# Attention and two dense layers on one core: four token blocks of 256 to 512 become three of 512, and the units are gone through to and fro

## The chip, the core and the metric

The kernel runs on one core of one Trainium2 chip. The core has TensorE (PE: matrix products, into PSUM), VectorE (DVE), ScalarE (ACT), GpSimd (POOL) and SyncE (SP, which issues the transfers). The time of a run is device microseconds from the first to the last instruction of the program and what lies around it. Three runs of the kernel before took 701.15 to 702.93 us, median 701.39.

## What is computed

Attention over a sliding window with a few sink tokens, then two dense layers over the same 1536 tokens:

```
q, k, v: (2, 8, 768, 64)            # batch, heads, tokens, head size
scores = q k^T / 8                  # kept: first n_sink = 4 keys, and the last window = 128 keys
x  = softmax(scores) v              # -> 1536 tokens x 512
h  = x @ w_in1                      # 512 x 2048
g  = (a0 + a1 h + a2 h^2 + a3 h^3) / (1 + |b0||h| + |b1|h^2 + 1e-6)
x2 = g @ w_out1                     # 2048 x 512
h  = x2 @ w_in2                     # layer 2, the same sizes
out = (h * sigmoid(1.702 h)) @ w_out2
```

The weights arrive as 64-bit floats.

## The kernel before

**Tiling.** The tokens are cut into blocks T0 to T3 (`TB`, line 31) of 256, 384, 384 and 512 tokens; a block is a list of 128-token query blocks of one or two sequences. The 2048 hidden columns are 16 chunks of 128 in two halves of 8 (`HALVES`). A unit is one layer `m`, one block and one half (`UNITS`, line 35): for each layer, first half with T0 to T3, then second half with T0 to T3, 16 units in all. A step is as many chunks as fill 512 columns of the block: two chunks for T0, one for the others.

**A step.** `g1` (first products) makes `h` = x w_in for the chunk: 12 products per chunk, since operands are split in a high and a low part (`xh`, `xl`; a weight tile `wi` or `wo` holds both parts of one chunk). `el_a` and `el_b` turn `h` into `gh` and `gl` on ScalarE and VectorE: in layer 1 with seven VectorE operations (tiles `s`, `z`, `gh`, `gl`; the one that writes `gl` is the last), in layer 2 with two. `g2` (second products) adds the chunk's share of g w_out to four accumulators `acc`: in layer 1 again 12 products as wide as the block, in layer 2 with tokens as rows and always 512 columns wide. `g2` of a step follows `g1` of the third step after it (`LAG`).

**Partial sums.** A unit sees 8 of 16 chunks. At its end `finish` copies the four accumulators to a tile `xf`; after the second half they are added to `xf` on VectorE, and the sum is split into the next layer's `xh` and `xl` or sent out. If the unit is the block's only one in that layer (`part is None` at the last unit), the accumulators are copied once to a tile of tag `r`, and nothing is added.

**Weights.** 64 weight tiles (16 chunks, `wi` and `wo`, two layers) are transferred into two buffers `wraw` and decoded from 64-bit by `decode`: on VectorE five operations a tile (`dy`, two kinds of `dt`, and the one that writes the low part of `wi` or `wo`), on ScalarE one or two. There are 8 slots each for `wi` and `wo` and one more once attention is over, so a chunk of the next half can be decoded only when the last product with an old chunk frees its slot. I call the block with which that happens the turning block: T3 before, for both turns within a layer and for the turn between layers.

**Attention.** `attention(T, ...)` makes the layer-1 input of block T, head by head: scores on TensorE (`k`,`q`), masks and maxima on VectorE (`m`, `nm`), exponentials on ScalarE, normalisation on GpSimd, transposes (`ident`,`a`) and values (`th`,`vr`) on TensorE. The first product of layer 1 needs all 8 heads of T0. Until then, and while TensorE's list has holes, the planner puts in fillers: products with a tile of zeros (line 844), 110 of them, beside 20 at the start (line 565).

**Order.** All operations go through one planner (`Program.play`), which fixes the order on every engine when the program is built: each operation has a cost, the one with the longest tail goes first, and `BIAS`, `HEAD` and `THETA` (numbers per category of operation) shift that. TensorE, VectorE, ScalarE, GpSimd and SyncE then run their lists strictly in that order.

Of the kernel before, what the change touches and what calls it, by code (L numbers as in the profile page):

```python
# [27 lines left out]
LN2_64 = 64.0 * 0.6931471805599453  # L28


TB = [[(0, [0, 1])], [(0, [2, 3, 4])], [(0, [5]), (1, [0, 1])], [(1, [2, 3, 4, 5])]]
XF_EARLY = (0, 1)

HALVES = [list(range(NF // 2)), list(range(NF // 2, NF))]
UNITS = [(m, T, fs) for m in (0, 1) for fs in HALVES for T in range(len(TB))]
GROUP = 3
LAG = 3

# [7 lines left out]
TH, SN, PE_OUT = "act/dve", "pool/dve", "act/dve"  # L46

BIAS = {
# [3 lines left out]
}  # L52
HEAD = (0.46, 1.43, 4.3, 7.1)
THETA = 1.27

WARM, FILL, FILL_AHEAD = 20, 6000, 0.1

# [4 lines left out]

START, PE_START, TICK, TICK_COLUMNS = 5.75, 6.25, 10.24 / 3, 3060
PE_LAT = 0.2
COL_FIX, COL_EACH = 0.4, 0.0275
TABLE = 1.3
LAT = 0.16
DMA_LAT, DMA_RATE, DMA_MIN = 1.9, 0.36e6, 65536
# [69 lines left out]
class Program:  # L138
# [139 lines left out]
    def play(self):  # L278
# [92 lines left out]
        def spares(o, e):  # L371
# [3 lines left out]
            for t, i in own[p]:  # L375
                if t >= -o.prio:
                    break
                q += ops[i].alts[p][0]
            return max(free[p], now) + q + o.alts[p][0] > now + o.alts[e][0] + THETA

# [112 lines left out]
def emit(tc, qT, kX, vL, w_in, w_out, ca, cb, nw, out):  # L493
    nc = tc.nc
    R = Program(nc, tc)
# [12 lines left out]
    def hi(eng, o, i):  # L508
        l = eng.split("/")
        return one_of([form(e, o, i) for e in l])  # L510
# [28 lines left out]
    pre_w = {("wraw", j): cst.tile([P, 512, 2], I32, name=f"wraw_{j}") for j in range(RAW_BUFS)}  # L539
    (b0, l0), = TB[0]  # L540
    n0 = len(l0)
# [78 lines left out]
    def moe(pools, blocks, units, x1_ready, late_pool):  # L620
# [153 lines left out]
        def finish(u, m, T, c, a, nt):  # L774
            w = nt if m == 0 else 512
            part = xf.get((m, T, c))
            if u != last_unit[m, T]:
                if part is None:
                    if (m, T) not in xf:
                        early = T in XF_EARLY  # L780
                        xf[m, T] = R.tile(xp if early else get_late, [P, KC * nt], F32, tag=f"xf{T}", name="xf", bufs=1, late=not early)
# [46 lines left out]
    def build_banded():  # L828
        with (
# [22 lines left out]
            def attention(T, xs, alone):  # L852

                parts = TB[T]
                qs = [(b, qb) for b, l in parts for qb in l]
# [30 lines left out]
                for k in sorted(kbs, key=lambda k: -len(near[k])) + (["s"] if sq else []):  # L886
                    w = len(near[k]) if k != "s" else 1
# [15 lines left out]
                def pst(kind):  # L903
                    if alone and kind == "s":
                        return R.tile(ps, [P, 512], F32, tag="acc", name="pss", bufs=4)
                    if alone and kind == "v":
                        return R.tile(ps, [P, 512], F32, tag="h", name="psv", bufs=H_BUFS)
                    return R.tile(ps, [P, 512], F32, tag="att", name="psa", bufs=8 - 4 - H_BUFS)
# [18 lines left out]
                def scores(h):  # L927

                    kr, qr = st.pop(("kq", h // 2))
                    t = []  # L930
                    for e in (h, h + 1):
                        a = R.tile(ap, [P, 4, 2 * P + SC], F32, tag="a", name="a", bufs=A_BUFS)
                        nm = R.tile(ap, [P, 4], F32, tag="nm", name="nm", bufs=5)
                        sm = R.tile(ap, [P, 4], F32, tag="sm", name="sm", bufs=5)
                        st["a", e] = a, sm
                        t.append((slice((e % 2) * D, (e % 2 + 1) * D), a, nm, sm))
                    for i, (b, qb) in enumerate(qs):
                        off, w = (P + SC, P) if qb == 0 else (0, 2 * P + SC)
                        k0 = kcol[b, max(0, qb - 1)] * KW
                        ps_ = [pst("s") for _ in t]  # L940
                        R.op("tensor", "matmul", alloc=[x for y in t for x in y[1:]], cost=w / 600 + 2 * COL_EACH, calls=[
                            dict(out=p[:, :w], lhsT=qr[r, i * P:(i + 1) * P], rhs=kr[r, k0:k0 + w], start=True, stop=True)
                            for p, (r, _, _, _) in zip(ps_, t)])
                        for p, (_, a, nm, sm) in zip(ps_, t):
                            mt = R.tile(ap, [P, 2 * P + SC], F32, tag="m", name="mt", bufs=M_BUFS)
                            R.op("vector", "tensor_tensor_reduce",
                                out=mt[:, :w], in0=p[:, :w], in1=mk[min(qb, 2)], scale=-SCALE, scalar=3.0e38,
                                op0=ALU.add, op1=ALU.min, accum_out=nm[:, i:i + 1])
                            R.op("scalar", "activation", out=a[:, i, off:off + w], in_=mt[:, :w], func=AF.Exp, scale=-1.0,
                                 bias=nm[:, i:i + 1], accum_out=sm[:, i:i + 1])  # L950
# [42 lines left out]
                def values(h):  # L993

                    x = pst("v")
                    calls, vrs = [], []
                    for e in (h, h + 1):
                        r0 = (e % 2) * D
                        p, tr, vr = x[r0:r0 + D], st.pop(("T", e)), st.pop(("v", e))
                        vrs.append(vr)  # L1000
                        ops = []
                        for k in first + later:
                            (g, at), n = place[k], len(near[k])
                            q0 = qcol[near[k][0]]
                            ops.append((p[:, q0 * P:(q0 + n) * P], vr[:, vcol[k], :], tr[g][:, at * P:(at + n) * P]))
                        for j, (o, l, r) in enumerate(ops):
                            calls.append(dict(out=o, lhsT=l, rhs=r, start=(j == 0), stop=(not sq and j == len(ops) - 1)))
                    if sq:
                        for e in (h, h + 1):
                            q0, n = qcol[sq[0]] * P, len(sq) * P  # L1010
                            calls.append(dict(out=x[(e % 2) * D:(e % 2 + 1) * D, q0:q0 + n], lhsT=vrs[e % 2][:SC, vcol[sq[0][0], "s"], :], rhs=st.pop(("sT", e))[:, :n], start=False, stop=True))
                    cost = COL_FIX + sum(c["rhs"].n / 1200 + COL_EACH for c in calls)
                    R.op("tensor", "matmul", calls=calls, cost=cost)
                    n, c = nq * P, h // 2
                    hi(XH, xs[0][c][:, :n], x[:, :n])
                    lo("dve", xs[1][c][:, :n], x[:, :n], xs[0][c][:, :n])
# [4 lines left out]
                def first_of(h):  # L1021
# [3 lines left out]
                    if h:  # L1025
                        R.follow(firsts[-2], firsts[-1], 2 * HEAD[T])

# [8 lines left out]

            moe((wp, xp, gp, tp, ps), TB, UNITS, attention, late_pool)
            held.pop().__exit__(None, None, None)

    def build_general():  # L1040
        with tc.tile_pool(name="xd", bufs=1, space=DRAM) as dp:
# [66 lines left out]
            with (  # L1108
# [8 lines left out]
                def x1_ready(T, xs, alone):  # L1117
                    n = sum(len(l) for _, l in TB[T]) * P
                    t0 = TB[T][0][0] * S + TB[T][0][1][0] * P

# [6 lines left out]

                moe((wp, xp, gp, tp, ps), TB, UNITS, x1_ready, lambda: xp)

# [49 lines left out]
```

## Time and profile before

| | |
|---|---|
| median of 3 runs | 701.39 us (701.15 to 702.93) |
| the profiled execution | 701.9 us, its span 700.1 us |
| mean granted TensorE clock | 0.985 |
| busy | PE 670.2, DVE 533.3, ACT 407.2, POOL 73.2 us |

The profile comes from one execution on the chip. A page gives busy time by engine, a strip of 40 slices, the chain of waits that ended last and the costliest groups of instructions; the timeline gives every instruction with its start and its length in us. Products overlap in the array, so their length (0.39 us for 512 columns) is more than the distance at which they follow each other, and a full row of overlapping products counts as busy whatever the distance is. The distance from start to start is therefore what a product costs in a stream, and the same holds for VectorE, whose instructions overlap by some 0.08 us. The windows view gives the busy time of each engine in a stretch, with the number of instructions, the granted clock as a share of 2.4 GHz, the share of the transfer engines and their GB/s.

### The profile page before, as it was taken

The numbers are of one execution on the slowest core, as the hardware profiler recorded it, in microseconds if no ns is written. First come the engines' busy times: TensorE is split into PE (matmuls) and PEld (weight loads), VectorE is DVE, ScalarE is ACT, GpSimd is POOL, SyncE is SP. The second block draws the span as 40 slices with busy tenths as digits, with TensorE's granted clock in tenths as the row PEclk, the third lists the DMA queues.
The fourth block names the chain that finished last, engine by engine and source line by source line (L and its number), as shares of the span: only waits on it lengthen the run. The fifth ranks groups of instructions, "written<-read, shape, count | busy, mean of one in ns | idle before, by whom it ended". The sixth has DMA issues, their size and how long they took to land.

```text
span 700.1 us, 10401 instructions
## 1 busy us (share of the span) xinstructions
PE 670.2 (96%) x3690; PEld 569.8 (81%) x3690; DVE 533.3 (76%) x1182; ACT 407.2 (58%) x894; POOL 73.2 (10%) x131
## 2 busy tenths in 40 slices
PE   8999989999999986799998999999999999999995
PEld 7677767877888865699997888988888898888874
DVE  7999899868759999999999999985278753222341
ACT  5899888967788665768585773543345432221220
POOL 4262452422200000000000000000000000000000
PEclk9999999999999997999999999999999999999999
DMA  5653554400001033300201011342023200000021
GB/s 170 212 171 109 157 156 137 154 26 1 24 0 31 31 118 111 106 27 8 84 0 32 1 58 63 121 141 70 1 91 120 91 31 16 0 16 1 15 76 65
DMA packets 26412, 49.75 MB, mean 71 GB/s; under 512 B 6384, under 2 KB 15088, under 8 KB 26352
## 3 DMA queue, kind: packets, MB, share of 16 engines
q1 hardware_dynamic: 26064, 49.00, 22.7%
q8 instruction: 31, 0.51, 0.3%
q14 instruction: 29, 0.24, 0.1%
q10 hardware_dynamic: 288, 0.00, 0.0%
HBM read 45.85 MB, written 3.15 MB: 70 GB/s over the span
## 4 chain that ended last, share of the span: by engine, by line
PE 82%; DVE 11%; ACT 3%; issue 1%; DMA 1%; POOL 1%; SPq 0%; DVEq 0%; POOLq 0%; ACTq 0%
PE att L209 32%; PE acc L209 25%; PE h L209 20%; PE att L210 3%; DVE dt L210 2%; DVE s L210 2%; DVE z L210 2%; PE acc L844 1%; DVE gh L210 1%; POOL a L210 1%; DVE dy L210 1%; DMA q<-q_t 1%; DVE wi L210 1%; DVE gl L210 1%; DVE m L210 1%
## 5 line engine op out<-in xcount | busy, mean ns | idle before, releaser
L209 PE MATMUL h<-xh,wi 128*128 128x384 f32 (+2 forms) x608 | 168.7, 342 | 7.2 <-DVE s L210 7.2
L209 PEld LDWEIGHTS h<-xh,wi 128*128 128x128 f32 x608 | 110.3, 193 | 21.7 <-DVE s L210 9.4
L209 PE MATMUL att<-xh,wi 128*128 128x384 f32 (+2 forms) x416 | 116.7, 343 | 0.6 <-DVE s L210 0.6
L209 PE MATMUL acc<-gh,wo 128*128 128x384 f32 (+2 forms) x384 | 105.7, 342 | 0.0
L209 PE MATMUL h<-xl,wi 128*128 128x384 f32 (+2 forms) x304 | 102.8, 338 | 0.0
L210 DVE TENSOR_TENSOR gl<-y,gh 128x384 fp32r<-128x384 f32 (+1 forms) x56 | 33.8, 613 | 82.1 <-PE acc L209 41.3
L209 PE MATMUL acc<-wo,gh 128*128 128x512 f32 x288 | 93.7, 395 | 0.0
L210 DVE SCALAR_TENSOR_TENSOR dt<-wraw,dt 128x512 int32<-128x512 int32 x128 | 89.0, 696 | 0.6
L209 PEld LDWEIGHTS att<-xh,wi 128*128 128x128 f32 x416 | 75.2, 188 | 7.6 <-DVE s L210 0.9
L210 ACT ACTIVATE gh<-y 128x384 fp32r<-128x384 f32 (+1 forms) x56 | 31.5, 569 | 75.9 <-PE acc L209 39.7
L209 PEld LDWEIGHTS acc<-gh,wo 128*128 128x128 f32 x384 | 69.2, 192 | 5.8 <-issue 2.0
L209 PE MATMUL att<-xl,wi 128*128 128x384 f32 (+2 forms) x208 | 71.4, 343 | 0.0
L210 POOL TENSOR_SCALAR a<-a,rs 128x272 f32<-128x272 f32 (+1 forms) x92 | 58.0, 647 | 109.2 <-DVE rs L210 71.8
L209 PE MATMUL acc<-gl,wo 128*128 128x384 f32 (+2 forms) x192 | 62.9, 341 | 5.9 <-DVE gl L210 5.9
L209 PEld LDWEIGHTS acc<-wo,gh 128*128 128x128 f32 x288 | 53.3, 188 | 10.4 <-ACT xf L210 0.4
L209 PEld LDWEIGHTS h<-xl,wi 128*128 128x128 f32 x304 | 58.7, 193 | 3.4 <-issue 0.4
L210 ACT ACTIVATE dy<-wraw 128x512 f32<-128x512 f32 x64 | 42.9, 670 | 25.8 <-DMA wraw<-w_out 14.1
L209 PE MATMUL acc<-wo,gl 128*128 128x512 f32 x144 | 52.7, 394 | 0.0
L210 ACT ACTIVATE a<-m,nm 128x272 f32<-128x272 f32 (+1 forms) x96 | 47.2, 493 | 5.5 <-DVE nm L210 4.7
L210 ACT ACTIVATE r<-z,ln_b 128x384 f32<-128x384 f32 (+1 forms) x56 | 37.0, 660 | 16.0 <-DVE z L210 15.8
L209 PEld LDWEIGHTS acc<-gl,wo 128*128 128x128 f32 x192 | 36.2, 192 | 10.1 <-DVE gl L210 7.8
L209 PE MATMUL att<-gh,wo 128*128 128x512 f32 (+2 forms) x128 | 40.8, 359 | 1.2 <-ACT xf L210 1.2
(118 smaller groups left out, 1234.4 us busy)
## 6 DMA issues: line engine op xcount, KB each, us to landing
wraw<-w_in SPq DMA_DIRECT2D x32, 512.0 KB, 3.6
wraw<-w_out SPq DMA_DIRECT2D x32, 512.0 KB, 3.5
out<-xf SPq DMA_DIRECT2D x12, 256.0 KB, 2.3
k<-k_x SPq DMA_DIRECT2D x12, 144.0 KB, 2.7
vr<-v_l SPq DMA_DIRECT2D x24, 64.0 KB, 2.5
k<-k_x SPq DMA_DIRECT2D x4, 360.0 KB, 3.6
vr<-v_l SPq DMA_DIRECT2D x8, 160.0 KB, 2.5
k<-k_x SPq DMA_DIRECT2D x4, 288.0 KB, 4.4
```

The lines of the kernel that those rows point to most:

```text
L209: return getattr(e, meth)(a.pop("out"), **a)
L210: return getattr(e, meth)(**a)
L844: nc.tensor.matmul(R.real[k][:, 0:256], lhsT=zero[:, :P], rhs=zero, start=True, stop=True)
```

## The change

The blocks become three of 512 tokens: T0 is the first four query blocks of the first sequence, T1 its last two and the first two of the second sequence, T2 the last four. Every step is now one chunk wide 512 columns; there are 96 steps instead of 112. The units go to and fro: in layer 1 T0, T1 with the first half, T2 with all 16 chunks in one unit, T1, T0 with the second half; in layer 2 T2, T1 with the first half, T0 with all 16, T1, T2 with the second half. Ten units instead of 16; T2 in layer 1 and T0 in layer 2 are units without partial sums, and they are the turning blocks of their layers. `XF_EARLY` (which blocks' `xf` lies in memory that is there from the start) becomes T0 alone. All numbers of `BIAS`, `HEAD` and `THETA` are new, and three costs that the planner assumes for attention's products; these shift the order on every engine.

```
-TB = [[(0, [0, 1])], [(0, [2, 3, 4])], [(0, [5]), (1, [0, 1])], [(1, [2, 3, 4, 5])]]
-XF_EARLY = (0, 1)
+TB = [[(0, [0, 1, 2, 3])], [(0, [4, 5]), (1, [0, 1])], [(1, [2, 3, 4, 5])]]
+XF_EARLY = (0,)
 HALVES = [list(range(NF // 2)), list(range(NF // 2, NF))]
-UNITS = [(m, T, fs) for m in (0, 1) for fs in HALVES for T in range(len(TB))]
+LAST = len(TB) - 1
+THERE, BACK = list(range(LAST)), list(range(LAST - 1, -1, -1))
+UNITS = ([(0, T, HALVES[0]) for T in THERE] + [(0, LAST, HALVES[0] + HALVES[1])] + [(0, T, HALVES[1]) for T in BACK]
+         + [(1, T, HALVES[0]) for T in [LAST] + BACK[:-1]] + [(1, 0, HALVES[0] + HALVES[1])] + [(1, T, HALVES[1]) for T in THERE[1:] + [LAST]])
 BIAS = {
-    "at0": 15.33, "at1": 21.93, "at2": 26.03, "at3": 6.7, "m0": -10.71, "m1": -2.77, "m2": -0.5,
+    "at0": 73.99, "at1": -22.55, "at2": 69.14, "at3": 10.82, "m0": -20.57, "m1": -1.79, "m2": 85.22,
...
-HEAD = (0.46, 1.43, 4.3, 7.1)
-THETA = 1.27
+HEAD = (1.41, 3.84, 7.97, 14.15)
+THETA = 1.19
...
-COL_FIX, COL_EACH = 0.4, 0.0275
+COL_EACH = 0.1
...
-                        R.op("tensor", "matmul", alloc=[x for y in t for x in y[1:]], cost=w / 600 + 2 * COL_EACH, calls=[
+                        R.op("tensor", "matmul", alloc=[x for y in t for x in y[1:]], cost=w / 420 + 0.11, calls=[
...
-                    cost = COL_FIX + sum(c["rhs"].n / 1200 + COL_EACH for c in calls)
+                    cost = sum(c["rhs"].n / 1100 + COL_EACH for c in calls)
```

TensorE's list around the first product of layer 1 (`h` from `xh_0`, `wi`), before; `th`, `vr` are attention's values, `k`, `q` its scores, `zero` the fillers:

```order
L209 MATMUL h_324<-th_315,vr_200 64x256
L209 MATMUL h_324<-th_315,vr_200 64x128
L209 MATMUL att_294<-k_60,q_61 128x272
L209 MATMUL att_275<-k_60,q_61 128x272
L844 MATMUL acc_187<-zero 128x256 x5
L209 MATMUL att_322<-k_181,q_184 128x272
L209 MATMUL att_294<-k_181,q_184 128x272
L844 MATMUL acc_187<-zero 128x256
L209 MATMUL h_324<-xh_0_0_340,wi_302 128x256
```

and now:

```order
L214 MATMUL h_448<-th_405,vr_198 64x256
L214 MATMUL h_448<-th_422,vr_198 64x256
L214 MATMUL h_448<-th_428,vr_198 64x256
L214 MATMUL h_448<-th_405,vr_198 64x128
L214 MATMUL h_448<-sT_386,vr_194 64x256
L214 MATMUL h_448<-sT_419,vr_198 64x256
L214 MATMUL att_359<-k_60,q_61 128x272
L214 MATMUL att_357<-k_60,q_61 128x272
L849 MATMUL acc_187<-zero 128x256 x7
L214 MATMUL h_448<-xh_0_0_474,wi_279 128x512
```

The first product is row 78 of TensorE's list before and row 155 now; the values of a head pair ahead of it have eight rows and two for the sink keys where they had four, it is 512 columns wide instead of 256, and 132 fillers stand ahead of it instead of 71.

VectorE's list ahead of the last `gl` of the block that precedes the first turning block, before (T2, its eighth chunk); `dy`, `dt`, `wi` and `wo` on the left are decoding:

```order
L210 TENSOR_TENSOR wi_302<-dt_298,wi_302 128x512
L210 TENSOR_TENSOR s_2348<-s_2348,h_324 128x512
L210 SCALAR_TENSOR_TENSOR dt_239<-wraw_64,dt_239 128x512
L210 SCALAR_TENSOR_TENSOR s_2348<-s_2348,a_t,h_324 128x512
L210 TENSOR_SCALAR dt_298<-dy_243 128x512
L210 SCALAR_TENSOR_TENSOR gh_1075<-s_661,a_t,r_691 128x384
L210 TENSOR_TENSOR z_792<-z_792,y_2369 128x512
L210 SCALAR_TENSOR_TENSOR z_647<-z_647,gh_1075 128x384
L210 TENSOR_TENSOR s_801<-s_801,att_275 128x512
L210 SCALAR_TENSOR_TENSOR s_661<-s_661,a_t,z_647 128x384
L210 SCALAR_TENSOR_TENSOR s_801<-s_801,a_t,att_275 128x512
L210 TENSOR_TENSOR gl_1114<-s_661,r_691 128x384
```

and now (T1, its eighth chunk):

```order
L215 SCALAR_TENSOR_TENSOR dt_232<-wraw_64,dt_232 128x512
L215 TENSOR_TENSOR wi_438<-dt_288,wi_438 128x512
L215 TENSOR_SCALAR dy_235<-dy_235 128x512
L215 TENSOR_SCALAR dt_288<-dy_235 128x512
L215 TENSOR_TENSOR wo_2254<-dt_232,wo_2254 128x512
L215 SCALAR_TENSOR_TENSOR dt_288<-wraw_65,dt_288 128x512 x2
L215 SCALAR_TENSOR_TENSOR gh_980<-s_864,a_t,r_884 128x512
L215 SCALAR_TENSOR_TENSOR z_855<-z_855,gh_980 128x512
L215 TENSOR_SCALAR dy_218<-dy_218 128x512
L215 SCALAR_TENSOR_TENSOR s_864<-s_864,a_t,z_855 128x512
L215 TENSOR_SCALAR dt_232<-dy_218 128x512
L215 TENSOR_TENSOR gl_1019<-s_864,r_884 128x512
```

Ahead of that `gl` VectorE's list has 111 decode operations now and 96 before, since the tiles of the second half begin to be decoded earlier against the chunks of the first half.

TensorE's list where the second half begins, before (T3's last second products, then T0's first product with chunk 8):

```order
L209 MATMUL att_294<-gl_807,wo_1349 128x512
L209 MATMUL att_294<-gh_2301,wo_1349 128x512
L209 MATMUL att_322<-gl_807,wo_1349 128x512
L209 MATMUL att_322<-gh_2301,wo_1349 128x512
L209 MATMUL h_324<-xh_0_0_340,wi_2299 128x256
L209 MATMUL h_324<-xl_0_0_348,wi_2299 128x256
```

and now (T2 goes on with the same `xh`, `xl`):

```order
L214 MATMUL h_448<-xh_3_0_2048,wi_876 128x512
L214 MATMUL att_357<-gh_980,wo_1075 128x512
L214 MATMUL acc_191<-gh_1065,wo_1088 128x512
L214 MATMUL att_353<-xh_0_0_1665,wi_2066 128x512
L214 MATMUL att_353<-xl_0_0_1680,wi_2066 128x512
L214 MATMUL att_353<-xh_1_0_1818,wi_2066 128x512
```

The block does not change there any more, and a chunk of the second half meets 512 columns where it met 256.

## Rows read from the trace of the kernel before

**Rows 1.** The page: busy time by engine, and the chain that ended last.

```profile
PE 670.2 (96%) x3690; PEld 569.8 (81%) x3690; DVE 533.3 (76%) x1182; ACT 407.2 (58%) x894; POOL 73.2 (10%) x131
...
PE 82%; DVE 11%; ACT 3%; issue 1%; DMA 1%; POOL 1%; SPq 0%; DVEq 0%; POOLq 0%; ACTq 0%
```

**Rows 2.** Windows of four stretches: length, busy by engine, clock, transfers' share, GB/s.

```profile
0.00:33.90 33.90, 31.18 (x199) 23.27 (x200) 27.43 (x116) 23.11 (x72) 11.97 (x26) 1.00 0.62 187
33.90:233.80 199.90, 195.95 (x1236) 157.46 (x1237) 169.79 (x451) 164.23 (x436) 58.66 (x102) 0.99 0.30 89
233.80:430.50 196.70, 180.67 (x976) 163.26 (x975) 194.65 (x362) 129.35 (x220) 2.62 (x3) 0.97 0.16 50
430.50:700.10 269.60, 262.42 (x1284) 225.86 (x1282) 141.47 (x257) 90.50 (x168) 0.00 (x0) 0.99 0.18 59
```

**Rows 3.** Timeline of TensorE, three landmarks: start, length, engine, line, operation.

```profile
33.95 0.28 PE L209 MATMUL h<-xh,wi 128*128 128x256 f32 x1
...
233.84 0.33 PE L209 MATMUL acc<-gh,wo 128*128 128x384 f32 x1
...
430.49 0.39 PE L209 MATMUL acc<-gl,wo 128*128 128x512 f32 x1
```

**Rows 4.** Timeline of TensorE: products in a stream, three widths.

```profile
520.48 0.39 PE L209 MATMUL h<-xl,wi 128*128 128x512 f32 x1
...
521.84 0.39 PE L209 MATMUL h<-xl,wi 128*128 128x512 f32 x1
...
140.12 0.33 PE L209 MATMUL h<-xl,wi 128*128 128x384 f32 x1
...
141.16 0.33 PE L209 MATMUL h<-xl,wi 128*128 128x384 f32 x1
...
35.99 0.29 PE L209 MATMUL h<-xl,wi 128*128 128x256 f32 x1
...
36.70 0.28 PE L209 MATMUL h<-xl,wi 128*128 128x256 f32 x1
```

**Rows 5.** Windows of 20 us: PE, PEld, DVE, ACT, POOL, clock, transfers, GB/s.

```profile
180.00:200.00 20.00, 19.86 (x126) 15.75 (x126) 11.10 (x28) 15.73 (x42) 4.56 (x9) 1.00 0.01 1
...
260.00:280.00 20.00, 11.62 (x55) 10.05 (x56) 19.98 (x38) 11.73 (x20) 0.00 (x0) 0.75 0.39 120
280.00:300.00 20.00, 15.92 (x97) 14.09 (x97) 19.87 (x36) 14.93 (x26) 0.00 (x0) 0.93 0.37 117
```

**Rows 6.** Timeline of VectorE at A and B.

```profile
225.04 0.55 DVE L210 TENSOR_TENSOR gl<-s,r 128x384 fp32r<-128x384 f32 x1
...
428.66 0.69 DVE L210 TENSOR_TENSOR gl<-s,r 128x512 fp32r<-128x512 f32 x1
```

**Rows 7.** Timeline of VectorE: operations in a stream, 512 and 384 columns.

```profile
233.72 0.69 DVE L210 TENSOR_TENSOR wi<-dt,wi 128x512 fp32r<-128x512 f32 x1
234.32 0.42 DVE L210 TENSOR_SCALAR dy<-dy 128x512 f32<-128x512 f32 x1
234.66 0.68 DVE L210 TENSOR_TENSOR s<-s,att 128x512 f32<-128x512 f32 x1
...
244.10 0.74 DVE L210 SCALAR_TENSOR_TENSOR s<-s,a_t,h 128x512 f32<-128x512 f32 x1
244.76 0.69 DVE L210 TENSOR_TENSOR gl<-s,r 128x512 fp32r<-128x512 f32 x1
...
206.85 0.61 DVE L210 SCALAR_TENSOR_TENSOR gh<-s,a_t,r 128x384 fp32r<-128x384 f32 x1
207.38 0.55 DVE L210 TENSOR_TENSOR z<-z,y 128x384 f32<-128x384 f32 x1
207.85 0.55 DVE L210 SCALAR_TENSOR_TENSOR z<-z,gh 128x384 f32<-128x384 f32 x1
```

**Rows 8.** The fillers' group: busy, mean ns, idle time before them.

```profile
L844 PE MATMUL acc<-zero 128*128 128x256 f32 x110 | 20.5, 309 | 0.1
```

5 rows, old and new, of the table BIAS are left out of this document.

## The prediction

> **What bounds the kernel now.** I read the busy shares and the chain of waits first [rows 1]: TensorE is busy 96% of the span and carries 82% of the chain that ended last, VectorE carries 11%. That makes TensorE the bound on average, so the next question is where TensorE waits, and for whom. The table of four stretches [rows 2] answers it. They are cut at three landmarks [rows 3]: the first product of layer 1 (33.95), point A (233.84: the second product of the last chunk of the block that precedes the turning block T3) and point B (430.49: the second product of the last chunk of layer 1). Between A and B VectorE is busy 194.65 of 196.7 us and TensorE 180.67; before A and after B VectorE has idle time, and TensorE is all but full.
>
> A busy TensorE is not yet a TensorE at its pace, so I price its list by the distance from start to start. Six products lie between the two rows of each width in [rows 4]: 1.36/6 = 0.227 us at 512 columns, 1.04/6 = 0.173 at 384, 0.71/6 = 0.119 at 256. The list of before has, from A to B, 309 products of 512 columns, 399 of 384 and 264 of 256: 70.1 + 69.0 + 31.4 = 171 us. They took 196.7. So TensorE lost 25.5 us there, most of it at 260 to 300, where it is busy 11.62 and 15.92 of 20 us and the granted clock falls to 0.75 [rows 5].
>
> VectorE's list for the same work, from the g of that chunk to the last g of layer 1 (225.04 to 428.66, [rows 6]), is priced the same way [rows 7]: 0.60 us for an operation on two tensors of 512 columns, 0.66 where it also reads a scalar per partition, 0.34 for a plain scalar operation, 0.53 and 0.47 at 384. One chunk then costs 4 x 0.60 + 3 x 0.66 = 4.38 us at 512 columns and 3.47 at 384; decoding one weight tile is 2 x 0.34 + 3 x 0.60 = 2.48. The list holds 20 chunk steps of 512 and 16 of 384, less 6 operations that stand ahead of it (139.6), 99 decode operations (49.2), 24 partial-sum adds and splits and a cast (10.4) and 1.2 of layer 2: 200.3 us, against 203.6 by the trace. **So A to B is VectorE's stretch; the rest is TensorE's.** This is what the prediction rests on.
>
> **The change, part by part.** I count the changed order over the same three landmarks; A is now the last chunk of T1's first half, B the last of T0's second half.
>
> *Start to A, TensorE.* Before: 63, 369 and 192 products of 512, 384 and 256 columns, 14.3 + 63.8 + 22.8 = 101 us; after, 420 of 512, 95.3. Attention has the same work (440 rows against 432), and it falls into 24 passes of a head and a block instead of 32. The fillers go from 110 to 162 [rows 8]; at the 256-column pace each is 0.12 us: +6.2. Sum: -5.6 + 6.2 = **+0.6 us**. What the list does not show is the waits: A came at 233.84 with 201 us of list, so about 33 were lost. The added wait is at the first product: it needs all 8 heads of four query blocks instead of two, and 132 fillers stand ahead of it instead of 71. Its list is 47 us long instead of 24.5, so I expect it at 57 to 61 us, not 34. Behind it in TensorE's queue stands only attention of T1; nothing of layer 1 could start anyway. Bounds on this wait: the lost time up to there was 33.95 - 24.5 = 9.5; at worst it grows with the list (x 47/24.5 = 18, +9); at best the 23 lost between 34 and 234 shrink with the share of attention that is still open at the first product, from 5/6 to 2/3 (-5). I take 0, since the attention itself is the same.
>
> *Start to A, VectorE.* 15 more decode operations stand here (111 instead of 96, three tiles, +7.4), and 6.5 in all. The cover is VectorE's idle time: it is busy 11.10 of 20 us at 180 to 200 [rows 5], and its list to A is 180 of 225 us. If that cover were gone, it would cost its 6.5.
>
> *A to B, VectorE.* 32 chunk steps of 512, less 6 operations: 136.9 (-2.7); 84 decode operations, 42.0 (-7.2, the three tiles that moved ahead of A); 4 adds and 8 splits, 7.2 (-3.2: T2 needs no partial sum, and T0's adds now fall behind B); 0.6 of layer 2. Sum 186.8, that is **-13.5 us**. TensorE's list there is 756 x 0.227 = 172 us, the same as before; it still does not bind. Next in line is therefore still VectorE, with 15 us more than TensorE instead of 29. Bounds: at least nothing (the same 16 + 16 tiles must be decoded somewhere), at most all 25.5 that TensorE lost. ScalarE was busy 129.35 of 196.7 [rows 2], and its operations on a chunk only become fewer and wider; it does not become the bound.
>
> *B to the end, TensorE.* Before 204 x 0.227 + 384 x 0.173 + 120 x 0.119 = 127.0 us of first products, after 554 x 0.227 = 125.8, and two second products fewer (0.5): **-1.7**. VectorE is busy 141.47 of 269.6 there, so the adds that go (T0 of layer 2 is one unit) give nothing, and the four result tiles of T0 that now share a buffer with other work wait behind their output transfers under that cover. The closing steps, four adds and four transfers of T2's 512 tokens, are those of T3 before: 0. The transfer queue has the same 64 weight loads and 76 attention loads instead of 104: 0.
>
> Sum: 701.9 + 0.6 - 13.5 - 1.7 = **687.3 us** in the measure of the profiled execution, which is 0.5 above the median of the runs: 687.
>
> A rule that speaks against a part of this: a product of 512 columns follows the last at 227 ns [rows 4], 13 ns more than its columns take at 2.4 GHz, and those at 384 and 256 columns show the same 13; so each product that is not issued saves some 13 ns. The Trainium skill, TensorE: Matmul & The Clock Gate, section Back-to-back issue gap, gives about 2.5 ns beyond the columns for a lone warm product. By that, 204 fewer products ahead of A and 154 fewer behind B would give back 3.8 us of the sum, 691 in all, an estimate; that is the edge of my forecast's own range. The trace's spacing, at three widths, does not agree with it, so it gets no chance of its own.
>
> **The rivals.** *Half the turn.* The three tiles that moved ahead of A need chunk slots that TensorE's first products of the turning block free; if VectorE reaches them late, the 7.2 us come back after A, and only 2.7 + 3.2 + 0.4 of the list are gained. For it: the order keeps VectorE and TensorE within a few us of each other for the whole of A to B, so small slips on either side add up. Against: VectorE's idle 45 us before A. Time: 701.9 + 0.6 - 6.3 - 1.7 = 694.5.
>
> *The whole turn.* TensorE waits for nothing between A and B, since at 512 columns a chunk is 24 x 0.227 = 5.45 us of TensorE against 4.38 of VectorE. Then 701.9 + 0.6 - 25.5 - 1.7 = 675. Against: 186.8 is still more than 172.
>
> *Nothing moves.* The turn gives its certain 6.3, and the start takes 9: 701.9 + 0.6 + 9 - 6.3 - 1.7 = 703.5; with a start of +5, 699.5.
>
> *A dearer start, slower.* VectorE is late at A, because the attention of four query blocks stands ahead of the first chunk and the decoding falls in behind it. Then the first product costs its upper bound (+9), the 6.5 of VectorE are not covered, and the turn, whose tiles are late as well, gains only its 6.3: 701.9 + 0.6 + 9 + 6.5 - 6.3 - 1.7 = 710. It passes the time of before when A is some 9.5 us later than I expect, at 244. For it: until the first product TensorE already spent about half its time on fillers and waits (71 x 0.12 + 9.5 of 34 us), and that phase nearly doubles. Against: VectorE's list to A is 187 us of 234.
>
> That the change does not do what it says can be left out: the changed order has 8 partial-sum copies and 8 adds in each layer, where layer 1 had 16 and 16 and layer 2 had 12 and 12, and the four results of each turning block are copied out once.
>
> **How the numbers follow.** My forecast, 681 to 691: 0.50. Half the turn, 691 to 699: 0.25. The whole turn, below 681: 0.08. Nothing moves: 0.06. Slower: 0.11. A difference of 0.3%, 2.1 us, is about what a measurement of this kernel can tell from none; so faster 0.83, same 0.06, slower 0.11. The range takes in the forecast, half the turn and most of the whole turn: 678 to 699.
>
> **What would show it.** The first product at 57 to 61 us; A at 230 to 238; A to B 178 to 188 us, with VectorE busy over 97% of it and no 20 us in which TensorE's granted clock falls to 0.75; B to the end 268. The prediction is wrong if A comes later than 243 (the start was dearer), if A to B takes over 190 (the decoded tiles came late), or if ScalarE or a weight transfer is what VectorE waits for between A and B.

## The result and the profile after

The changed kernel took 696.26 us (median of 5 runs, 693.99 to 696.68), the kernel before, measured beside it, 701.39 (700.96 to 703.0): ratio 0.9912, 95% interval 0.9887 to 0.9938. That is 6.2 us less by the ratio. The forecast was 14.4 us less. The time lies in the stated range (678 to 699), above the forecast's own 681 to 691, and nearest to the rival *half the turn* (694.5).

The page of the changed kernel, busy time by engine and chain, for [rows 1]:

```profile
PE 670.9 (97%) x3150; PEld 519.4 (75%) x3150; DVE 524.0 (75%) x1086; ACT 396.3 (57%) x827; POOL 70.2 (10%) x118
...
PE 81%; DVE 8%; ACT 5%; DMA 3%; issue 1%; SPq 0%; ACTq 0%
```

Fewer VectorE operations, less of VectorE on the chain, and TensorE as full as before: the page doesn't tell where the missing 8 us are (14.4 less 6.2). The stretches between the landmarks do. Columns as in [rows 2]; the lines of the landmarks stand under it, and of two or three products in one line the last is meant (236.86, 425.92).

```profile
0.00:66.20 66.20, 60.91 (x376) 44.44 (x377) 54.20 (x189) 45.62 (x142) 17.32 (x37) 0.95 0.58 175
66.20:236.90 170.70, 168.91 (x894) 121.03 (x893) 143.37 (x346) 135.70 (x336) 49.04 (x77) 1.00 0.26 76
236.90:425.90 189.00, 180.39 (x757) 144.16 (x756) 186.88 (x313) 124.51 (x195) 3.86 (x4) 0.97 0.15 46
425.90:694.30 268.40, 260.68 (x1128) 209.73 (x1126) 139.56 (x241) 90.48 (x154) 0.00 (x0) 0.99 0.19 59
```

```profile
66.23 0.42 PE L214 MATMUL h<-xh,wi 128*128 128x512 f32 x1
...
236.63 0.62 PE L214 MATMUL acc<-gl,wo 128*128 128x512 f32 x2
...
425.46 0.84 PE L214 MATMUL acc<-gh,wo 128*128 128x512 f32 x3
```

| stretch | before | expected change | after | change |
|---|---|---|---|---|
| start to A | 233.84 | +0.6 | 236.86 | +3.0 |
| A to B | 196.65 | -13.5 | 189.06 | -7.6 |
| B to the end of the span | 269.6 | -1.7 | 268.4 | -1.2 |
| span | 700.1 | -14.6 | 694.3 | -5.8 |

Of what is missing, two thirds lie between A and B and a quarter ahead of A. The same shows on VectorE: the `gl` that precedes A, and the last of layer 1.

```profile
234.75 0.68 DVE L215 TENSOR_TENSOR gl<-s,r 128x512 fp32r<-128x512 f32 x1
...
425.75 0.67 DVE L215 TENSOR_TENSOR gl<-s,r 128x512 fp32r<-128x512 f32 x1
```

Between the two VectorE took 191.0 us where it had taken 203.6 [rows 6]: 12.6 less, nearly the 13.5 of the sum. But it stood at the first of them 9.7 us later (225.04 before), and TensorE only 3.0 later, so VectorE entered the turn with a lead of 2.1 us over TensorE in place of 8.8. And TensorE still starves, later than in [rows 5]:

```profile
280.00:300.00 20.00, 18.45 (x81) 14.74 (x79) 20.00 (x35) 10.06 (x16) 0.00 (x0) 1.00 0.00 1
300.00:320.00 20.00, 15.16 (x45) 11.40 (x46) 19.26 (x35) 11.17 (x19) 0.00 (x0) 0.74 0.38 111
```

In the second row TensorE starts 45 products in 20 us, at a granted clock of 0.74 (a mean of its two levels, 1.2 and 2.4 GHz), and VectorE is all but full. The products it waits for there (in brackets the idle time and what ended it):

```profile
301.03 0.50 PE L214 MATMUL acc<-gh,wo 128*128 128x512 f32 x1 [2.58 <-ACT wo L215]
...
310.93 0.50 PE L214 MATMUL h<-xh,wi 128*128 128x512 f32 x1 [2.54 <-ACT wi L215]
```

Both wait for a weight tile of the second half, the one for its `wo`, the other for its `wi`, and in both cases for ScalarE, which makes the tile's high part. All of TensorE's waits from A to B (us in total, times, the longest):

```profile
PE acc L214 <- ACT wo L215: 2.6, 1, 2.6
PE h L214 <- ACT wi L215: 2.5, 1, 2.5
PE att L214 <- DVE gl L215: 2.0, 2, 1.8
PE att L214 <- DVE s L215: 1.4, 2, 1.3
```

The same view of the kernel before, from A to B:

```profile
PE h L209 <- DVE s L210: 7.2, 3, 5.9
PE acc L209 <- DVE gl L210: 5.2, 4, 2.8
PE att L209 <- DVE gl L210: 1.9, 1, 1.9
PE att L209 <- ACT xf L210: 1.2, 2, 0.7
PE att L209 <- DVE s L210: 0.6, 1, 0.6
```

The waits for VectorE went from 14.9 us to 3.4, those for ScalarE from 1.2 to 5.1.

In what follows, "TensorE lost" is worked out as in the prediction: the start of a product less the list ahead of it at the prices of [rows 4]. Ahead of A it also needs prices for attention's products, which no row shows; differences between kernels hold there to about 1 us.

### The profile page after: what moved, and what is told of

It reads as the page before. It is cut to its first block, busy times and chain, and to the rows that moved or that the text cites. A ratio compares the mean times of both kernels' runs of the same rounds, so it can differ in the third digit from the quotient of the medians.

```text
span 694.3 us, 9046 instructions
## 1 busy us (share of the span) xinstructions
PE 670.9 (97%) x3150; PEld 519.4 (75%) x3150; DVE 524.0 (75%) x1086; ACT 396.3 (57%) x827; POOL 70.2 (10%) x118
## 4 chain that ended last, share of the span: by engine, by line
PE 81%; DVE 8%; ACT 5%; DMA 3%; issue 1%; SPq 0%; ACTq 0%
PE att L214 31%; PE acc L214 25%; PE h L214 20%; PE acc L849 3%; DVE s L215 3%; DMA wraw<-w_out 2%; PE att L215 2%; DVE z L215 2%; DVE dt L215 1%; DMA q<-q_t 1%; ACT th L215 1%; DVE gh L215 1%; ACT y L215 1%; ACT r L215 1%; ACT sT L215 1%
## 5 line engine op out<-in xcount | busy, mean ns | idle before, releaser
L214 PE MATMUL h<-xh,wi 128*128 128x512 f32 x432 | 148.4, 401 | 3.3 <-ACT wi L215 2.5
L214 PE MATMUL att<-xh,wi 128*128 128x512 f32 x336 | 111.8, 393 | 1.4 <-DVE s L215 1.4
L214 PE MATMUL acc<-gh,wo 128*128 128x512 f32 x288 | 101.8, 403 | 2.6 <-ACT wo L215 2.6
L215 DVE TENSOR_TENSOR gl<-y,gh 128x512 fp32r<-128x512 f32 x48 | 32.6, 688 | 85.7 <-PE acc L214 44.5
L214 PE MATMUL h<-xl,wi 128*128 128x512 f32 x216 | 85.9, 398 | 0.0
L215 ACT ACTIVATE dy<-wraw 128x512 f32<-128x512 f32 x64 | 42.7, 668 | 40.3 <-DMA wraw<-w_out 26.1
L214 PE MATMUL att<-xl,wi 128*128 128x512 f32 x168 | 65.7, 391 | 0.0
L214 PE MATMUL acc<-gl,wo 128*128 128x512 f32 x144 | 56.0, 403 | 0.0
L214 PE MATMUL att<-wo,gh 128*128 128x512 f32 x128 | 47.3, 395 | 0.0
L215 ACT ACTIVATE r<-z,ln_b 128x512 f32<-128x512 f32 x48 | 34.5, 721 | 13.7 <-DVE z L215 13.3
L215 DVE TENSOR_TENSOR z<-z,y 128x512 f32<-128x512 f32 x48 | 33.2, 692 | 7.7 <-ACT z L215 7.5
```

The source lines that it names most:

```text
L214: return getattr(e, meth)(a.pop("out"), **a)
L215: return getattr(e, meth)(**a)
```

## The experiments

Two questions: is the start dearer because of TensorE's clock, its fillers or VectorE; and is the turn set by the amount of VectorE's work? Ratios are against the kernel before on the same chip, with their 95% interval; the changed kernel has 0.9912.

**The start: the clock.** In the first 20 us of the changed kernel TensorE waits for the first `q`, which now has 512 columns, and then runs at a lower clock (windows of 10 us; then, from the timeline, the first score):

```profile
0.00:10.00 10.00, 6.47 (x30) 5.68 (x32) 4.38 (x27) 2.45 (x7) 2.05 (x11) 0.92 0.62 200
10.00:20.00 10.00, 10.00 (x54) 7.04 (x55) 7.04 (x30) 6.28 (x22) 0.95 (x2) 0.74 0.51 154
```

```profile
8.21 0.65 PE L214 MATMUL acc<-k,q 64*128 64x128 f32 x4 [2.02 <-DMA q<-q_t]
```

`warm40`:

```
-WARM, FILL, FILL_AHEAD = 20, 6000, 0.1
+WARM, FILL, FILL_AHEAD = 40, 6000, 0.1
```

> The changed kernel with 40 products on zeros at its very start in place of 20, all else in its own order. In the changed kernel TensorE waits 2.02 us for the first q (8.21 us) and then works at a clock of 0.74 from 10 to 20 us; the kernel before had 1.00 there. Theory A (the dearer start is this cold clock): the clock stays at 1.00, the first product of layer 1 comes 2 to 3 us earlier than 66.2, and the time falls by 2 to 3 us. Theory B (the start is the chain of attention through VectorE, ScalarE and the transfers, and TensorE fills up with fillers): the clock is repaired, the first product and the time move by less than 1 us.

692.89 us, ratio 0.9874 (0.9845 to 0.9904). The same windows, the first score and the first product:

```profile
0.00:10.00 10.00, 8.66 (x50) 8.10 (x52) 4.48 (x27) 2.30 (x7) 2.05 (x11) 1.00 0.61 200
10.00:20.00 10.00, 10.00 (x69) 7.28 (x69) 9.26 (x38) 7.79 (x29) 3.35 (x6) 1.00 0.62 193
```

```profile
8.74 0.49 PE L214 MATMUL acc<-k,q 64*128 64x128 f32 x4
...
62.98 0.42 PE L214 MATMUL h<-xh,wi 128*128 128x512 f32 x1
```

The first score comes half a us later (8.74), and yet TensorE starts 69 products from 10 to 20 us where it had 54, VectorE is busy 9.26 in place of 7.04, and the first product comes 3.2 us earlier. A and B follow by 3.3 and 4.8 us in this trace (233.5, 421.1), the median by 3.4, or 2.7 by the ratios. The intervals of the two ratios overlap, and the profiled run is the fastest of its four (690.64; the others 692.72 to 693.32), so the time alone does not settle it. The place does: the 25th of attention's products, fillers not counted, starts at 17.91 in place of 20.32, so 2.4 us are gained by the end of the stretch with the low clock. Theory A holds: about 3 us of the time are the cold clock at the start.

The control, `b_warm40`, is the same edit in the kernel before.

> The kernel before in its own order with 40 products on zeros at the start in place of 20. Its clock is 1.00 in the first 20 us already. If the 3 us that the 40 products gave the changed kernel are the cure of its own cold start, the kernel before gains nothing (0 to 2 us slower, since the products end after its first q has come). If 40 products are better in general, it gains 2 to 3 us as well.

702.36 us, ratio 1.0015 (0.9999 to 1.0030). The kernel before was warm without it, and its first score moves from 6.89 to 9.59. So the gain of `warm40` belongs to the change: its first transfers are larger (256 KB for `q` instead of 128) and outlast the 20 products.

**The start: the fillers.** `fill_none`:

```
 def filler():
+    return
```

> The changed kernel in its own order, with the 162 fillers left out (they compute nothing that is used). 132 of them, 16 us of TensorE, stand ahead of the first product of layer 1. If the fillers stand in TensorE's way (my +6.2 in the start), the first product comes 4 to 10 us earlier and the time falls by 2 to 6 us. If they only fill holes, the first product stays within 1 us where the clock holds; where the clock falls without them, the first product comes later, by up to 10 us, and the time with it.

697.14 us, ratio 0.9924 (0.9896 to 0.9953): no difference in the whole time. Two windows of 20 us and the first product:

```profile
0.00:20.00 20.00, 15.13 (x52) 10.45 (x52) 13.81 (x65) 10.49 (x34) 5.67 (x17) 0.72 0.61 196
20.00:40.00 20.00, 18.24 (x78) 10.80 (x78) 16.62 (x59) 15.27 (x52) 4.88 (x9) 0.67 0.55 162
```

```profile
65.91 0.50 PE L214 MATMUL h<-xh,wi 128*128 128x512 f32 x1 [0.79 <-DVE xl L215]
```

Without fillers the clock stays at 0.72 and 0.67 for 40 us, and the first product comes 0.3 us earlier all the same. Two effects cancel in that sum, as the starts of attention's own products on TensorE show (us, fillers not counted):

| kernel | 25th | 121st | first product of layer 1 |
|---|---|---|---|
| changed | 20.32 | 41.08 | 66.23 |
| `warm40` | 17.91 | 38.65 | 62.98 |
| `fill_none` | 15.95 | 43.09 | 65.91 |

At the 25th the kernel without fillers is 4.4 us ahead of the changed one: at the low clock the fillers stood in the way. From there to the first product of layer 1 it takes 50.0 us where `warm40`, at full clock and with its fillers, takes 45.1, so the low clock takes the lead away again. No run leaves the fillers out at full clock; what they cost there is not shown.

The Trainium skill, TensorE: Matmul & The Clock Gate, section HAM oscillation — how this bites in real kernels, prices a cold stretch at its length times the share of the clock that is missing. By that, an estimate, the 10 us at 0.74 in the changed kernel cost 2.6 us, and the trace agrees: 2.4 at the 25th product. For `fill_none` it gives 20 x 0.28 + 20 x 0.33 = 12 us; what the trace shows, the 50.0 us above less the 45.1, is 4.9, and in that the missing fillers may have saved something, so this run does not test it.

**The start: VectorE.** `less_start` leaves an operation of decoding to the planner, at its cost, but does not issue it, so every list keeps its order:

```
-R.op("vector", "scalar_tensor_tensor", out=t, in0=lw, scalar=29, in1=t, ...)
+o = R.op("vector", "scalar_tensor_tensor", out=t, in0=lw, scalar=29, in1=t, ...)
+if R.cat in ("wi00", "wo00"):
+    o.alts = {e: (c, lambda: None) for e, (c, _) in o.alts.items()}
```

> The changed kernel in its own order, with the same operation left out for the 16 tiles of the first half of layer 1 (9.6 us of VectorE between 14 and 112 us). If VectorE sets the start (it is busy 9.0 to 9.97 of each 10 us from 20 to 66 us), the first product of layer 1 comes 5 to 7 us earlier and the time falls by as much. If the start is TensorE's list with the attention's chain of waits, the first product moves by less than 2 us and the time by 0 to 2.

693.60 us, ratio 0.9885 (0.9857 to 0.9913). The first stretch and the first product:

```profile
0.00:66.20 66.20, 61.96 (x382) 45.54 (x383) 49.24 (x183) 46.24 (x145) 16.12 (x37) 0.95 0.59 177
```

```profile
64.97 0.42 PE L214 MATMUL h<-xh,wi 128*128 128x512 f32 x1
```

VectorE has 5.0 us less to do (49.24 against 54.20), and the first product comes 1.3 us earlier; in `more_turn` and `less_turn` below, with this start unchanged, it came at 65.41 and 65.58, so 0.4 to 1.3 us are the edit's. The time is 1.9 us less by the ratios, whose intervals overlap. The second expectation holds: the amount of VectorE's work does not set the start.

**The turn: the amount of VectorE's work.** `less_turn` is the same edit for `("wi01", "wo01")`, `b_less_turn` that in the kernel before; `more_turn` issues the operation twice:

```
+if R.cat in ("wi01", "wo01"):
+    o.alts = {e: (c, lambda f=f: [f(), f()][-1]) for e, (c, f) in o.alts.items()}
```

> The changed kernel in its own order, with one VectorE operation of decoding (the one that adds the three lowest bits, 0.60 us) left out for the 16 tiles of the second half of layer 1; the lowest bits of those weights are then zero. 14 of the 16 operations stand between 207 and 327 us, where VectorE is busy without a pause. Theory 1 (the turn is VectorE's: the decoding of the second half starts only when the turning block's products free slots, so it is not covered by VectorE's earlier idle time): 14 x 0.60 = 8.4 us less, 6 to 9 us by the clock of TensorE that fills up; 687 to 690. Theory 2 (the turn waits for transfers of raw tiles or for ScalarE, and VectorE is only busy beside it): at most 2 us less. Theory 3 (what was lost lies at the start alone): 0.

> The changed kernel in its own order, with the same VectorE operation done twice for the same 16 tiles (14 x 0.60 = 8.4 us more in the turn). Theory 1: 7 to 10 us more, 703 to 706. Theory 2: 0 to 3 more. Theory 3: 0 to 2 more, since TensorE's list from A to B has 17 us of slack against its time.

> The kernel before in its own order, with the same operation left out for the 16 tiles of the second half of layer 1. 14 of them stand between 218 and 295 us. Theory 1: the turn was VectorE's before the change too, 6 to 9 us less, 692 to 695, and more than the changed kernel gains only if its turn was bound more tightly. Theory 2 and 3: 0 to 2 less.

| kernel | us | ratio | TensorE lost from 230 to 430 us |
|---|---|---|---|
| changed | 696.26 | 0.9912 (0.9887 to 0.9938) | 17.8 |
| `less_turn` | 695.49 | 0.9907 (0.9878 to 0.9936) | 16.6 |
| `more_turn` | 706.11 | 1.0056 (1.0033 to 1.0079) | 25.9 |
| before | | 1 | 26.1 |
| `b_less_turn` | 699.39 | 0.9970 (0.9953 to 0.9987) | 23.3 |

8.4 us more cost 10, as Theory 1 has it; TensorE lost 8.1 more in this stretch and 2 ahead of it. 8.4 us less brought 0.4 by the ratio, as Theory 2 and 3 have it. In the kernel before the same cut brought 2. No single theory stands. The windows of 207 to 345 us tell what became of the cut; the changed kernel, `less_turn` and `more_turn`, each from its own trace:

```profile
207.00:345.00 138.00, 131.29 (x546) 104.63 (x545) 135.98 (x230) 92.46 (x145) 3.32 (x4) 0.96 0.18 54
```

```profile
207.00:345.00 138.00, 132.13 (x560) 106.11 (x559) 130.72 (x222) 94.31 (x149) 3.35 (x4) 0.98 0.19 58
```

```profile
207.00:345.00 138.00, 125.69 (x508) 98.54 (x507) 136.24 (x228) 87.04 (x137) 3.53 (x4) 0.94 0.18 54
```

VectorE was full with 135.98 of 138 us. The cut turned into idle time of VectorE (130.72), and TensorE got 14 more products into that time. The reason is seen at TensorE's wait of 2.58 us ahead of 301.03. In the changed kernel VectorE's last three operations on raw tiles ahead of it, and ScalarE's rows:

```profile
298.43 1.89 DVE L215 SCALAR_TENSOR_TENSOR dt<-wraw,dt 128x512 int32<-128x512 int32 x3
```

```profile
298.49 0.69 ACT L215 ACTIVATE y<-h,ab 128x512 f32<-128x512 f32 x1 [5.72 <-PE h L214]
299.08 0.68 ACT L215 ACTIVATE z<-h,sb 128x512 f32<-128x512 f32 x1
299.65 0.78 ACT L215 ACTIVATE s<-h,a_t 128x512 f32<-128x512 f32 x1
300.35 0.63 ACT L215 ACTIVATE wo<-dt 128x512 fp32r<-128x512 f32 x1
```

The same place in `less_turn`, VectorE, ScalarE and TensorE:

```profile
297.27 0.69 DVE L215 SCALAR_TENSOR_TENSOR dt<-wraw,dt 128x512 int32<-128x512 int32 x1
```

```profile
297.30 0.69 ACT L215 ACTIVATE y<-h,ab 128x512 f32<-128x512 f32 x1 [5.68 <-PE h L214]
297.88 0.68 ACT L215 ACTIVATE z<-h,sb 128x512 f32<-128x512 f32 x1
298.45 0.78 ACT L215 ACTIVATE s<-h,a_t 128x512 f32<-128x512 f32 x1
299.12 0.64 ACT L215 ACTIVATE wo<-dt 128x512 fp32r<-128x512 f32 x1
```

```profile
296.88 0.39 PE L214 MATMUL h<-xh,wi 128*128 128x512 f32 x1
299.81 0.80 PE L214 MATMUL acc<-gh,wo 128*128 128x512 f32 x1 [2.54 <-ACT wo L215]
```

The cast that makes `wo` stands in ScalarE's list behind three operations on an `h` that TensorE has only just finished. In the changed kernel decoding ends at 300.32 and ScalarE's list is through with the three at the same time: the cast starts at 300.35. In `less_turn` two of VectorE's three operations are gone and decoding ends at 297.96; the cast still starts only at 299.12, behind the three. TensorE waits 2.54 us, as long as in the changed kernel, for a ScalarE that has itself waited 5.68 us for TensorE. So at this place two chains end together: VectorE's decoding, and the round from TensorE through ScalarE's list back to TensorE. Shortening VectorE's leaves the other; lengthening it lengthens the wait (4.04 us in `more_turn`). ScalarE's round was neither shortened nor lengthened.

At the second wait (ahead of 310.93) the round alone ends last, in the changed kernel already:

```profile
308.29 0.68 DVE L215 SCALAR_TENSOR_TENSOR dt<-wraw,dt 128x512 int32<-128x512 int32 x1
```

```profile
310.24 0.64 ACT L215 ACTIVATE wi<-dt 128x512 fp32r<-128x512 f32 x1
```

This is VectorE's last operation on a raw tile ahead of the cast of `wi`. It ends at 308.97, and the cast starts at 310.24, again behind three operations on a product that TensorE has just finished. Which chain ends last at the other waits was not taken apart, nor whether the transfers of raw tiles, for which ScalarE waits 7.4 us between 207 and 345 us, reach TensorE.

**The numbers, the size and the turn.** The change has three parts: blocks, order of units, numbers of the planner. To part them, four kernels got numbers by one and the same search: numbers were tried until the planner's own account of the program ended early. The planner's costs are those of the changed kernel; those with three blocks have 40 products at the start, so that none starts cold. The edits, besides `BIAS` and `THETA`:

```
 p_toFro3:     TB and UNITS of the changed kernel
 p_straight3:  +UNITS = [(m, T, fs) for m in (0, 1) for fs in HALVES for T in range(len(TB))]
 p_straight4:  TB and UNITS of the kernel before
 p_toFro4:     +UNITS = ([(0, T, HALVES[0]) for T in range(3)] + [(0, 3, HALVES[0] + HALVES[1])]
               +         + [(0, T, HALVES[1]) for T in (2, 1, 0)] + ...
```

> The blocks and the units of the changed kernel, with another set of planner numbers, found by the same search on the planner's own end of the program for all four kernels of this group, and 40 products on zeros at the start. It is the base of the group: 688 to 695 us, as the changed kernel with 40 products (692.9); the planner's own end is 661 against 665 for the changed kernel, so 689 if the planner is right to the us.

> Three blocks of 512, but units in the old order (first half T0 to T2, then second half T0 to T2), numbers by the same search, 40 products on zeros. If the gain is the blocks' size (204 fewer products ahead of A, wider VectorE operations), it stays within 4 us of the kernel that goes to and fro. If it is the way to and fro (no partial sums in the turning blocks, the turn on one block), it is 6 to 10 us slower than that kernel. The planner's own end is 664 against 661.

> The four blocks of the kernel before, gone through to and fro, numbers by the same search, 20 products on zeros. If the size makes the gain: as the four blocks in the old order, within 3 us. If the turn order makes it: 6 to 10 us faster than those. The planner's own end is 674 against 673.

> Blocks and units of the kernel before, numbers by the same search, 20 products on zeros. It tells what the numbers alone do: 698 to 706 if they matter by no more than 5 us. Against the three blocks in the old order: 7 to 12 us slower if the size makes the gain, within 3 us if not.

| kernel | us | ratio | TensorE lost up to 225 us | from there to 425 us |
|---|---|---|---|---|
| `p_straight4` | 697.54 | 0.9945 (0.9927 to 0.9964) | 32 | 22 |
| `p_toFro4` | 706.37 | 1.0073 (1.0045 to 1.0100) | 46 | 19 |
| `p_straight3` | 692.29 | 0.9853 (0.9831 to 0.9875) | 30 | 18 |
| `p_toFro3` | 687.86 | 0.9797 (0.9774 to 0.9820) | 32 | 12 |
| before | | 1 | 32 | 26 |
| changed | 696.26 | 0.9912 (0.9887 to 0.9938) | 35 | 18 |

- *The numbers alone* are worth 3.9 us in the kernel before (0.55%, `p_straight4`), and 5 us against `warm40` in the changed one. The whole change measured 6.2.
- *The size*: with three blocks in the old order of units the time is 5.3 us less. *To and fro* with three blocks takes off 4.4 more: TensorE loses 6 us less in the turn and 2 more ahead of it. Each kernel stands on the one set of numbers that its search found, and two sets for the same blocks and units differ by 4 to 5 us; so differences of this size are not shown to be the size's or the order's own.
- With four blocks the turn is some 2 us better when gone to and fro, as it should be, and the time 8.8 worse, since 14 us more are lost ahead of the turn. Where that loss comes from was not looked into, so this pair says nothing on the turn's worth with four blocks.

`p_toFro3` beats both kernels: 2.0% under the one before. From A to B (234.2 to 420.0) and in the windows of its turn:

```profile
234.20:420.00 185.80, 180.12 (x770) 142.94 (x769) 184.68 (x314) 127.95 (x200) 1.25 (x2) 1.00 0.15 46
280.00:300.00 20.00, 17.90 (x78) 14.03 (x76) 19.76 (x36) 13.83 (x23) 0.00 (x0) 1.00 0.21 65
300.00:320.00 20.00, 18.19 (x71) 12.79 (x72) 20.00 (x37) 12.22 (x21) 0.00 (x0) 1.00 0.29 94
```

VectorE is as full as in the changed kernel, but TensorE's waits are spread, 71 products start where 45 did, and the clock stays at 1.00. Blocks, units and TensorE's products of the layers are the same, in another order on the engines. The other engines share the rest a little otherwise: VectorE has 1112 operations instead of 1086, ScalarE 809 instead of 827, GpSimd 110 instead of 118, nearly all of it in attention.

Last, the cut of `less_turn` in this kernel's order, `p_less_turn`.

> The three blocks to and fro with the searched numbers (687.9), in that kernel's own order, with one VectorE operation of decoding (0.60 us) left out for the 16 tiles of the second half of layer 1; 14 of the 16 stand between 209 and 323 us, where VectorE is busy 99%. TensorE loses 10 us there. If the amount of VectorE's work sets the turn, TensorE loses 4 to 6 us less and the time is 682 to 684. If several chains (VectorE, ScalarE behind TensorE's own products, two buffers for raw tiles) are tied in the planned order, as in the changed kernel, where the same cut brought less than 1 us, the time stays within 2 us of 687.9 and VectorE gets idle instead.

684.40 us, ratio 0.9761 (0.9733 to 0.9789): 2.5 us less by the ratio, 3.5 by the medians. From 207 to 345 us VectorE is busy 132.72 in place of 136.90, and TensorE starts 13 products more:

```profile
207.00:345.00 138.00, 134.90 (x577) 108.48 (x576) 132.72 (x225) 100.52 (x159) 0.00 (x0) 0.99 0.18 54
```

Neither expectation: a third of the 8.4 us or a little more arrives, and TensorE's loss from 230 to 430 us falls from 12.4 to 10.0. It is more than in the changed kernel, by ratios whose intervals overlap, and far from one for one.

## Why the prediction was half right

Two steps failed. The wait at the start that I priced at 0 left out the cold clock (A came 2.4 us later than the sum had it), and VectorE's idle time ahead of A, which I took as a cover for the decoding that moved there, covered none of it (A to B took 5.9 us more than the sum had it).

**What held.** The direction, and the mechanism: A to B is where the gain lies, VectorE is full there (186.88 of 189.0 us, 98.9%), and its way from the `gl` at A to the last `gl` of layer 1 became 12.6 us shorter, where the sum had 13.5. B to the end came at 268.4 as said; the 0.5 us that are missing there can't tell 13 ns from 2.5 ns for a product not issued. The rule of the Trainium skill that I weighed for that (TensorE: Matmul & The Clock Gate, section Back-to-back issue gap) stays untested here. A came at 236.86, inside 230 to 238.

**Start to A, TensorE.** The step that failed is the wait that I priced at 0 between -5 and +9, "since the attention itself is the same". The first product came at 66.23, not at 57 to 61; TensorE had lost 19 us by then, twice the 9.5 of before, which is my worst end. About 3 us of it are the cold clock that `warm40` took away. I had counted the transfers (fewer, so 0) and not asked when the first one lands: `q` and `k` of the first block doubled, and the 20 products at the start no longer reached up to it. The rest was given back before A. The +6.2 for the fillers stays open: `fill_none` took the clock away with them.

**Start to A, VectorE.** "The cover is VectorE's idle time ... If that cover were gone, it would cost its 6.5." It was gone. VectorE stood idle 39.3 us ahead of that `gl` (before: 36.5 by the trace, 45 by my list), but all but 0.2 of it lies ahead of 207 us. Decoding stands still in that time (by the code, since all eight slots of each kind hold chunks of the first half until the turning block's products free them). Of the operations that read a raw tile, these two follow one another:

```profile
128.34 0.70 DVE L215 SCALAR_TENSOR_TENSOR dt<-wraw,dt 128x512 int32<-128x512 int32 x1
...
208.90 0.68 DVE L215 SCALAR_TENSOR_TENSOR dt<-wraw,dt 128x512 int32<-128x512 int32 x1
```

So the 15 operations that moved ahead of A stand where VectorE has no pause left, and none in its idle time. It reached the `gl` 9.7 us later: 3.3 of that is the start (in `warm40` it comes at 231.44), and the 6.4 left are about the 6.5 that moved ahead. `more_turn` confirms that work added there is not covered: four of its added operations, 2.4 us, stand ahead of that `gl`, and it comes at 238.21, 3.5 later. This is what I had put under *half the turn*, with a chance of 0.25; its price, 7.2 us come back, was about right: 5.9 are missing there.

**A to B.** The sum had -13.5, and -7.6 came. With the 6.7 us of lead that VectorE lost at A, the sum would have given -6.8. I had let a gain that was only moved across a landmark count in full. The bound that I drew from it was too simple as well: "VectorE's stretch" held for more work and not for less (`more_turn` +10, `less_turn` -0.4). A list that fills 99% of a stretch shows what the stretch can't go below, not that it is the only chain of that length. ScalarE, which I had ruled out by its busy time, holds TensorE up twice by the order of its list, 5.1 us in all. And I had expected no 20 us with the clock at 0.75: there was one, at 0.74.

**The term that I didn't have.** I counted lists and took the order in them as given. `p_toFro3` has the blocks, units and work of the changed kernel and takes 687.86, about the 687 that I forecast. So the work allows that time, with attention shared out a little otherwise, and of the 9.3 us between the changed kernel's median and 687, 3 are its cold start and 5 the way its planner's numbers set the lists against each other. That the number came out in the end with other lists is no merit of the sum.

**The rivals.** *A dearer start* did happen in a small way, and *nothing moves* and *the whole turn* did not: even in `p_toFro3` TensorE loses 12 us in the turn.

## To carry to other kernels

Cut a timeline at landmarks of the engine that binds, and book work that moves across a landmark on both sides: idle time ahead of it is a cover only where the moved work can really start in it. Where a planner has balanced the lists, as here, price added work in full and removed work at a fraction, and try other numbers for the planner before a change of structure is judged. When a first transfer grows, check that whatever keeps TensorE busy until then still reaches up to it.

## What had not been expected of the hardware

- A wait of 2.02 us at 6 us of the program was followed by a granted clock of 0.74 from 10 to 20 us, and that cost about 3 us of the whole time, although no product of a layer stands there. Twenty products more at the start removed it, though they let the first score begin 0.5 us later.
- Fillers at the low clock stand in the way: without them the 25th of attention's products started at 15.95 in place of 20.32. But then the clock stayed at 0.72 and 0.67 over 40 us, and the first product of layer 1 came at 65.91 against 66.23, so nothing was left of the lead.
- An engine that is busy 124.51 of 189.0 us held TensorE up for 5.1 us: ScalarE's cast of a weight tile stood behind three operations that could start only when TensorE had finished.
